# A ConvNeXt V2 block on one core: zero rows appended to the expansion matmul, and rstd transposed on VectorE instead of TensorE

## The chip, the core and the metric

The kernel runs on one core of a Trainium2 chip. The metric is device time in microseconds (us), lower is better. Engines are named as in the profile: PE is TensorE's matrix multiplication, PEld its weight loads, DVE is VectorE, ACT is ScalarE, POOL is GpSimd, SP is SyncE, and SPq is SP's sequencer, which issues most of the DMAs here. PEclk, or "the granted clock", is the share of full speed that TensorE's clock was granted: 0.5 is called cold here, 1.0 warm.

## The reference

One image of 512 x 512 pixels and 96 channels goes through a depthwise 3x3 convolution, a LayerNorm over channels, an expansion to 384, a GELU, a global response normalization (GRN) and a projection back.

```python
# x (1,512,512,96), dw (3,3,96), w1 (96,384), w2 (384,96), all bf16
out = depthwise_conv3x3(x, dw)                      # padding 1
h = _layernorm(out, axis=-1)                        # over the 96 channels
h = gelu(h @ w1)                                    # tanh form
gx = sqrt((h * h).sum(axis=(1, 2), keepdims=True) + 1e-6)
nx = gx / (gx.mean(axis=-1, keepdims=True) + 1e-6)
h = grn_gamma * (h * nx) + grn_beta + h
return x + h @ w2
```

GRN needs sums over the whole image, so the kernel has two phases: the first computes everything up to the GELU and its sums, the second projects. The change is in the first phase.

## The kernel before

The first phase works in slots, one block of four image rows per slot and 128 in all. These are the parts that matter (cuts are marked `# ...`).

Convolution, eviction and squares of block b. ACT evicts the nine-tap result and POOL squares it:

```python
nc.tensor.matmul(Y[32*j:32*j+32, i, ...], lhsT=Wd[32*i:32*i+32, t, :], rhs=xT[32*i:32*i+32, ...], ...)
# ...
nc.scalar.activation(out=y[:], in_=Y[:], func=ACTF.Identity)                # y_bf
nc.gpsimd.tensor_tensor(out=q[:], in0=y[:], in1=y[:], op=ALU.mult)          # ysq
```

LayerNorm statistics. Two slots later PE sums y (12 matmuls) and then the squares (12 matmuls) into one PSUM tile S per batch of eight blocks. After the eighth block DVE turns S into rstd by a chain of some 15 small operations, PE transposes rstd, DVE copies it out, and SP writes it to DRAM and reads it back broadcast over partitions (rbc):

```python
for src, h in ((ybf[b], 0), (ysq.pop(b), 1)):
    # ...
    nc.tensor.matmul(S[:, h, ...], lhsT=src[:, i, g*128:(g+1)*128], rhs=rowsel[:], ...)
# ... stage_chain(k): mean, nmsq, var, ri, three Newton steps (t_, rn) on DVE, then
nc.tensor.matmul(S[:N, 2, :], lhsT=rn[:, :N], rhs=ident_bf[:], start=True, stop=True)
nc.vector.tensor_copy(out=rt[:N, :], in_=S[:N, 2, :])
nc.sync.dma_start(out=r_dram[...], in_=rt[:N, :])
# ... stage_bcast(k), one slot later: 4 DMAs  rbc <- r_dram
```

Normalization and expansion. POOL multiplies by rstd, SP writes the result to DRAM and reads it transposed (ynT), PE expands it, ACT applies the GELU, and DVE collects the sums for GRN:

```python
nc.gpsimd.tensor_tensor(out=yn[:], in0=ybf.pop(b)[:], in1=rbcs[k][...].to_broadcast(...), op=ALU.mult)
nc.sync.dma_start(out=yn_dram[b], in_=yn[:]...)
# ...
for i in range(2):
    nc.tensor.matmul(U[:, i, :], lhsT=w1p[:, j*128:(j+1)*128], rhs=ynts[b][:, i0+i, :], start=True, stop=True)
nc.scalar.activation(out=perm_view(gt[:, :], i0, 2), in_=perm_src(U[:]), func=ACTF.Gelu_apprx_tanh)
# ... nc.vector.bn_stats(...) on gt
```

The schedule puts the statistics LAG_ST = 2 slots after the convolution, the norms LAG_NORM = 4 slots after a batch's last statistics, and the expansion LAG_MLP = 3 slots after the norm. Every sixteenth slot has a burst of filler matmuls, meant to warm the clock (`fill_tiles(7)`). A compile-time scheduler orders each engine's instructions within the limits of their dependencies, so the order on POOL and SP is not always that of the text.

Of the kernel before, what the change touches and what calls it, by code (L numbers as in the profile page):

```python
# [19 lines left out]
LAG_MLP = 3  # L20
FILL_FIRST = 16
FILL_EARLY = 6
REWARM = 16


def batches_of(nblk):
# [13 lines left out]
def kernel(  # L40
# [46 lines left out]
    def yn_src(q):  # L87

        return yn_dram[q].rearrange("(r c) (i w) -> c i r w", r=GR, i=NI).rearrange("c i r w -> (c i) r w")
# [41 lines left out]
    nc.vector.memset(ones_f[:], 1.0)  # L131
    eps_t = consts.tile([128, 1], f32, name="eps_t")
    nc.vector.memset(eps_t[:], GRN_EPS)
    w1p = consts.tile([C, E], bf16, name="w1p")
    with tc.tile_pool(name="w1ps", bufs=1, space=bass.MemoryType.PSUM) as w1ps, \
            tc.tile_pool(name="w1tmp", bufs=1) as w1tmp:
        cen = w1tmp.tile([C, C], bf16, name="cen")
        nc.vector.memset(cen[:], 1.0)
        w1m = w1ps.tile([C, E], f32, name="w1m")
        nc.tensor.matmul(w1m[:], lhsT=cen[:], rhs=w1_raw[:], start=True, stop=True)  # L140
        nc.vector.scalar_tensor_tensor(out=w1p[:], in0=w1m[:], scalar=-1.0 / C, in1=w1_raw[:],
                                       op0=ALU.mult, op1=ALU.add)

    NACC = (NBLK + 7) // 8
# [24 lines left out]
    def recompute_units(q, pspool, uname):  # L169
        if not is_recomp(q) or q in done_recomp:  # L170
            return []
        gts, ynt = grp[q]["gts"], grp[q]["ynt"]
        units = []
        for i0 in range(0, GR, 2):
            for j in range(NCH):
                def unit(i0=i0, j=j):
                    U = pspool.tile([128, 2, W], f32, name=uname)
                    for i in range(2):
                        nc.tensor.matmul(U[:, i, :], lhsT=w1p[:, j * 128:(j + 1) * 128],  # L179
                                         rhs=ynt[:, i0 + i, :], start=True, stop=True)  # L180
                    nc.scalar.activation(out=perm_view(gts[j][:, :], i0, 2), in_=perm_src(U[:]),  # L181
                                         func=ACTF.Gelu_apprx_tanh)
                units.append(unit)
        return units
# [4 lines left out]
    with ExitStack() as p1:  # L189
# [4 lines left out]
        rtpool = p1.enter_context(tc.tile_pool(name="rt", bufs=2))  # L194
        rbcpool = p1.enter_context(tc.tile_pool(name="rbc", bufs=3))
        ynpool = p1.enter_context(tc.tile_pool(name="yn", bufs=3))
        yntpool = p1.enter_context(tc.tile_pool(name="ynt", bufs=4))
        gpool = p1.enter_context(tc.tile_pool(name="g", bufs=7))
        bstpool = p1.enter_context(tc.tile_pool(name="bst", bufs=2))
        psY = p1.enter_context(tc.tile_pool(name="psY", bufs=1, space=bass.MemoryType.PSUM))  # L200
# [61 lines left out]
        def stage_stats(b):  # L262
            k = batch_of[b]
            b0, n = BATCHES[k]
            if b == b0:
                Ss[k] = psS.tile([128, 3, 128], f32, name="S")
            S = Ss[k]
            for src, h in ((ybf[b], 0), (ysq.pop(b), 1)):
                for g in range(NG):
                    c0 = (b - b0) * GR * NG + g  # L270
                    for i in range(NI):
                        nc.tensor.matmul(S[:, h, c0:c0 + (GR - 1) * NG + 1:NG],  # L272
                                         lhsT=src[:, i, g * 128:(g + 1) * 128], rhs=rowsel[:],
                                         start=(i == 0), stop=(i == NI - 1))

        def stage_chain(k):
            b0, n = BATCHES[k]
            N = n * GR * NG
            S = Ss[k]
            mean = small.tile([128, 128], f32, name="mean")  # L280
            nc.vector.tensor_scalar(out=mean[:, :N], in0=S[:, 0, :N], scalar1=1.0 / C, scalar2=None, op0=ALU.mult)
            nmsq = small.tile([128, 128], f32, name="nmsq")
            nc.vector.scalar_tensor_tensor(out=nmsq[:, :N], in0=mean[:, :N], scalar=-1.0, in1=mean[:, :N],  # L283
                                           op0=ALU.mult, op1=ALU.mult)
            var = small.tile([128, 128], f32, name="var")
            nc.vector.scalar_tensor_tensor(out=var[:, :N], in0=S[:, 1, :N], scalar=1.0 / C, in1=nmsq[:, :N],
                                           op0=ALU.mult, op1=ALU.add)
            nc.vector.tensor_scalar(out=var[:, :N], in0=var[:, :N], scalar1=0.0, scalar2=LN_EPS,
                                    op0=ALU.max, op1=ALU.add)
            ri = small.tile([128, 128], i32, name="ri")  # L290
            nc.vector.tensor_scalar(out=ri[:, :N], in0=var[:, :N].bitcast(i32), scalar1=1, scalar2=None,  # L291
                                    op0=ALU.arith_shift_right)
            nc.vector.tensor_scalar(out=ri[:, :N], in0=ri[:, :N], scalar1=-1, scalar2=0x5F3759DF,
                                    op0=ALU.mult, op1=ALU.add)
            rcur = ri[:, :N].bitcast(f32)
            rn = None
            for it in range(NEWTON_ITERS):
                t_ = small.tile([128, 128], f32, name="nt")
                nc.vector.scalar_tensor_tensor(out=t_[:, :N], in0=rcur, scalar=-0.5, in1=rcur,  # L299
                                               op0=ALU.mult, op1=ALU.mult)  # L300
                nc.vector.tensor_tensor(out=t_[:, :N], in0=t_[:, :N], in1=var[:, :N], op=ALU.mult)  # L301
                rn = small.tile([128, 128], bf16 if it == NEWTON_ITERS - 1 else f32,
                                name="rstd" if it == NEWTON_ITERS - 1 else "rn")
                nc.vector.scalar_tensor_tensor(out=rn[:, :N], in0=t_[:, :N], scalar=1.5, in1=rcur,  # L304
                                               op0=ALU.add, op1=ALU.mult)
                rcur = rn[:, :N]

            nc.tensor.matmul(S[:N, 2, :], lhsT=rn[:, :N], rhs=ident_bf[:], start=True, stop=True)  # L308
            rt = rtpool.tile([128, 128], bf16, name="rt")
            nc.vector.tensor_copy(out=rt[:N, :], in_=S[:N, 2, :])  # L310
            nc.sync.dma_start(out=r_dram[b0:b0 + n].rearrange("b r (g m) -> (b r g) m", g=NG), in_=rt[:N, :])
            Ss.pop(k)

        def stage_bcast(k):
            b0, n = BATCHES[k]
# [12 lines left out]
            nc.sync.dma_start(out=yn_dram[b], in_=yn[:].rearrange("p i w -> p (i w)"))  # L328

        def stage_read(b):  # L330
            t = yntpool.tile([C, GR, W], bf16, name="ynT")
            nc.sync.dma_start(out=t[:], in_=yn_src(b))
            ynts[b] = t

        bsts = {}
# [43 lines left out]
            for m in range(n):  # L379
                nc.tensor.matmul(U[:, m % 2, :], lhsT=zero[:, :128], rhs=zero[:], start=True, stop=True)  # L380

        def fill_tiles(n):
            U = psU.tile([128, 2, W], f32, name="U")
            for m in range(n):
                for i in range(2):
                    for j in range(4):
                        nc.tensor.matmul(U[32 * j:32 * j + 32, i, :], lhsT=zero[32 * i:32 * i + 32, :32],  # L387
                                         rhs=zero[32 * i:32 * i + 32, :], start=True, stop=True)


        at = {}

# [5 lines left out]
        for k, (b0, n) in enumerate(BATCHES):  # L398
            for b in range(b0, b0 + n):
                s = b + LAG_ST  # L400
                if b == b0:
                    s = max(s, last_stat_slot + 2)
                put(max(s, b + LAG_ST), ("stats", b))
                last_s = max(s, b + LAG_ST)
            last_stat_slot = last_s
            put(last_s, ("chain", k))
            put(last_s + 1, ("bcast", k))
            for b in range(b0, b0 + n):
                s = max(last_norm + 1, last_s + LAG_NORM)
                last_norm = s  # L410
                put(s, ("norm", b))
                put(s + 2, ("read", b))
                put(s + LAG_MLP, ("mlp", b))
                last_slot = s + LAG_MLP
                if b % 8 == 7 or b == NBLK - 1:
                    put(s + LAG_MLP, ("combine", b // 8))
# [4 lines left out]
        for s in range(last_slot + 1):  # L421
# [7 lines left out]
                stage_bcast(k)  # L429
            for b in get("norm"):  # L430
                stage_norm(b)
            units = []
            for b in get("mlp"):
                units += mlp_units(b)
# [7 lines left out]
            if not u:  # L442
                order += t
                if t:
                    order.append(lambda: fill(FILL_EARLY))
                order += stats
            elif s % REWARM == REWARM - 1 and t:
                order += u[:2] + t + [lambda: fill_tiles(7)] + u[2:4] + stats + u[4:]
            else:
                k = 0  # L450
                while u or t:
                    if u:
                        order.append(u.pop(0))
                    n = 2 - k % 2
                    order += t[:n]
                    t = t[n:]
                    if k == 1:
                        order += stats
                    k += 1
# [126 lines left out]
```

## Time and profile before

| | before |
|---|---|
| time, median of 2 runs | 2130.15 us (2129.92 to 2130.39) |
| profiled span, mean granted clock | 2121.6 us, 0.660 |
| first phase ends (start of the GRN sums) | 1536.7 us |
| second phase | 584.9 us (2121.6 less 1536.7) |
| mean expansion matmul | 610 ns |

These lines of the profile page are the span and three rows of the slices. The span is cut into 40 equal slices, and each digit is the busy share of a slice in tenths, or for PEclk the granted clock in tenths.

```profile
span 2121.6 us, 59634 instructions
...
PE   7888999999999999999999989998579999999998
...
DVE  4465767867776786777678677779968888888887
...
PEclk8576555555555555555555575555589999999999
```

For three quarters of the time PE is about 90% busy at half clock, while DVE has room. One line of the windows view, for the stretch from 200 to 1150 us of the first phase, gives it in numbers. Its columns are the stretch, its length, busy time of PE, PEld, DVE, ACT and POOL (with instructions), the granted clock, the DMA share and GB/s.

```profile
200.00:1150.00 950.00, 907.86 (x12058) 245.70 (x12058) 698.07 (x1228) 594.70 (x571) 473.93 (x164) 0.50 0.66 178
```

PE is busy 908 of 950 us at exactly half clock. These are three groups of instructions from the page: line, engine, operation, output and inputs, shapes and count, then busy time and the mean ns of one, then the engine's idle time before them and what ended it.

```profile
L355 DVE BATCH_NORM_STATS2 bst<-gt 128x6 f32<-128x512 bf16 x1536 | 944.8, 679 | 364.2 <-ACT gt L352 364.2
...
L347 PE MATMUL U<-ynT,w1p 96*128 96x512 bf16 x1536 | 755.7, 610 | 19.4 <-ACT gt L352 18.2
...
L257 POOL TENSOR_TENSOR ysq<-y_bf 128x1536 bf16<-128x1536 bf16 x128 | 351.9, 2751 | 584.4 <-ACT y_bf L254 584.4
```

The expansion uses 96 of the array's 128 rows ("96*128"). A square takes POOL 2.75 us, and a norm takes it 3.09 us.

The only long waits of PE in the first phase are for rstd, once per batch: the waits view has 17 of them, 81.6 us in total, the longest 9.2. The PE timeline shows one of them (start, duration, instruction, and in brackets the idle time before it and its cause):

```profile
1237.43 0.60 PE L347 MATMUL U<-ynT,w1p 96*128 96x512 bf16 x2
1247.21 0.29 PE L308 MATMUL S<-ident_bf,rstd 128*128 128x128 bf16 x1 [9.18 <-DVE rstd L304]
```

PE started no other matmul in between, so everything behind the transpose stood for 9.18 us.

### The profile page before, as it was taken

Reading aid. Unit: us, or ns where it says so; the run is one execution under the profiler, and the core shown is the slowest. Engines: PE = TensorE matmul, PEld = TensorE weight load, DVE = VectorE, ACT = ScalarE, POOL = GpSimd, SP = SyncE. Lnnn points to the kernel's source line nnn. Section 1 sums busy time; section 2 is a strip of 40 time slices with the busy share of each in tenths; the row PEclk is TensorE's granted clock in tenths of the full one; section 3 lists DMA queues with packets and bytes.
Section 4 is the critical chain, followed back from the end, with each engine's and each line's share of the span. In section 5 each row is a group of like instructions: output and inputs, shape, how many; then the busy total and the mean of one; then the engine's idle time right before and its main releaser. Section 6 shows DMA issues by size and latency. Waiting matters only on the chain.

```text
span 2121.6 us, 59634 instructions
## 1 busy us (share of the span) xinstructions
PE 1925.0 (91%) x26046; PEld 776.0 (37%) x26046; DVE 1588.6 (75%) x2645; ACT 1395.9 (66%) x1381; POOL 850.1 (40%) x463
## 2 busy tenths in 40 slices
PE   7888999999999999999999989998579999999998
PEld 3433222232222223222222322232156666666665
DVE  4465767867776786777678677779968888888887
ACT  1464666665666666566666666678568787878787
POOL 4537445373644537364453745624021111111110
PEclk8576555555555555555555575555589999999999
DMA  8668666674866667476665868436199999999996
GB/s 159 184 144 219 166 180 163 173 204 127 222 163 189 158 175 209 122 225 157 194 159 170 209 161 220 145 123 218 69 350 364 371 367 371 365 375 366 374 363 232
DMA packets 459861, 472.21 MB, mean 223 GB/s; under 512 B 285424, under 2 KB 381776, under 8 KB 459600
## 3 DMA queue, kind: packets, MB, share of 16 engines
q1 hardware_dynamic: 406992, 348.85, 56.7%
q0 software_dynamic: 20608, 88.09, 11.2%
q10 hardware_dynamic: 32000, 31.46, 4.8%
q8 instruction: 203, 3.33, 0.7%
q14 instruction: 58, 0.48, 0.1%
HBM read 224.55 MB, written 176.69 MB: 189 GB/s over the span
## 4 chain that ended last, share of the span: by engine, by line
PE 62%; DVE 17%; ACT 14%; DMA 3%; POOL 2%; issue 1%; SPq 0%; ACTq 0%; DVEq 0%; POOLq 0%
PE U L347 25%; PE Y L244 21%; ACT gl L181 12%; DVE bst L355 10%; PE O L535 8%; PE S L272 3%; DMA out_dram<-o_sb 2%; DVE rstd L304 2%; ACT gt L352 1%; POOL yn L326 1%; DVE nmsq L283 1%; PE U L387 1%; DVE nt L301 1%; DVE nt L299 1%; DVE ri L291 1%
## 5 line engine op out<-in xcount | busy, mean ns | idle before, releaser
L355 DVE BATCH_NORM_STATS2 bst<-gt 128x6 f32<-128x512 bf16 x1536 | 944.8, 679 | 364.2 <-ACT gt L352 364.2
L352 ACT ACTIVATE gt<-U 128x1024 bf16<-128x1024 f32 x768 | 770.3, 1027 | 478.1 <-PE U L347 346.5
L347 PE MATMUL U<-ynT,w1p 96*128 96x512 bf16 x1536 | 755.7, 610 | 19.4 <-ACT gt L352 18.2
L244 PE MATMUL Y<-xT,Wd 32*32 32x512 bf16 x13806 | 587.2, 587 | 3.3 <-DMA xT<-in_x_dram 2.8
L257 POOL TENSOR_TENSOR ysq<-y_bf 128x1536 bf16<-128x1536 bf16 x128 | 351.9, 2751 | 584.4 <-ACT y_bf L254 584.4
L326 POOL TENSOR_TENSOR yn<-y_bf,rbc 128x1536 bf16<-128x1536 bf16 x128 | 392.3, 3089 | 130.3 <-DMA yn_dram<-yn 75.4
L535 PE MATMUL O<-W2s,gl 128*128 128x96 bf16 x6096 | 350.4, 206 | 19.7 <-ACT gl L181 5.1
L535 PEld LDWEIGHTS <-gl 128*128 128x128 bf16 x6096 | 304.2, 97 | 140.3 <-ACT gl L181 54.0
L537 DVE TENSOR_TENSOR o_sb<-O,xb 128x384 bf16<-128x384 f32 x512 | 257.3, 552 | 100.1 <-PE O L535 98.2
L244 PEld LDWEIGHTS <-Wd 32*32 32x32 bf16 x13806 | 156.0, 101 | 434.6 <-issue 411.8
L347 PEld LDWEIGHTS <-w1p 96*128 96x128 bf16 x1536 | 130.0, 117 | 477.8 <-issue 471.2
L165 POOL DMA_DIRECT2D xr<-in_x_dram x127 | 68.6, 541 | 496.8 <-DVE xb L526 373.2
L254 ACT ACTIVATE y_bf<-Y 128x1536 bf16<-128x1536 f32 x128 | 185.0, 1445 | 99.8 <-PE Y L244 99.8
L526 DVE TENSOR_TENSOR xb<-xr,B2bc_f 128x1536 f32<-128x1536 bf16 x127 | 222.9, 1755 | 10.6 <-DMA xr<-in_x_dram 7.9
L179 PEld LDWEIGHTS <-w1p 96*128 96x128 bf16 x960 | 76.7, 98 | 88.6 <-issue 72.9
L272 PEld LDWEIGHTS <-y_bf 128*128 128x128 bf16 x1536 | 66.3, 108 | 60.0 <-issue 58.6
L308 PE MATMUL S<-ident_bf,rstd 128*128 128x128 bf16 (+2 forms) x18 | 5.2, 290 | 81.6 <-DVE rstd L304 81.6
L272 PE MATMUL S<-rowsel,ysq 128*128 128x4 bf16 x1536 | 59.7, 168 | 8.1 <-POOL ysq L257 7.6
L272 PE MATMUL S<-rowsel,y_bf 128*128 128x4 bf16 x1536 | 63.5, 170 | 1.1 <-issue 1.1
L272 PEld LDWEIGHTS <-ysq 128*128 128x128 bf16 x1536 | 51.0, 103 | 10.1 <-POOL ysq L257 7.9
L159 POOL DMA_DIRECT2D gl<-g_dram x71 | 37.6, 533 | 6.4 <-DVE W2s L500 3.6
L308 PEld LDWEIGHTS <-rstd 128*128 128x128 bf16 (+2 forms) x18 | 1.9, 108 | 95.1 <-DVE rstd L304 94.8
(1123 smaller groups left out, 1079.0 us busy)
## 6 DMA issues: line engine op xcount, KB each, us to landing
g_dram<-gt SPq DMA_DIRECT2D x144, 512.0 KB, 3.8
yn_dram<-yn SPq DMA_DIRECT2D x128, 384.0 KB, 4.0
ynT<-yn_dram SPq DMA_DIRECT2D x128, 384.0 KB, 4.2
out_dram<-o_sb SPq DMA_DIRECT2D x128, 384.0 KB, 6.7
xr<-in_x_dram POOLq DMA_DIRECT2D x127, 384.0 KB, 7.0
gl<-g_dram POOLq DMA_DIRECT2D x71, 512.0 KB, 8.9
gl<-g_dram SPq DMA_DIRECT2D x70, 512.0 KB, 8.7
ynl<-yn_dram ACTq DMA_DIRECT2D x80, 384.0 KB, 9.9
```

What stands on the lines that cost most here:

```text
L181: nc.scalar.activation(out=perm_view(gts[j][:, :], i0, 2), in_=perm_src(U[:]), func=ACTF.Gelu_apprx_tanh)
L244: nc.tensor.matmul(Y[32 * j:32 * j + 32, i, oc0:oc1], lhsT=Wd[32 * i:32 * i + 32, t, :], rhs=xT[32 * i:32 * i + 32, r % XR, oc0 + dx:oc1 + ...
L254: nc.scalar.activation(out=y[:], in_=Y[:], func=ACTF.Identity)
L257: nc.gpsimd.tensor_tensor(out=q[:], in0=y[:], in1=y[:], op=ALU.mult)
L272: nc.tensor.matmul(S[:, h, c0:c0 + (GR - 1) * NG + 1:NG], lhsT=src[:, i, g * 128:(g + 1) * 128], rhs=rowsel[:], start=(i == 0), stop=(i == ...
L326: nc.gpsimd.tensor_tensor(out=yn[:], in0=ybf.pop(b)[:], in1=rbcs[k][:, b - b0:b - b0 + 1, :].to_broadcast([128, NI, W]), op=ALU.mult)
L347: nc.tensor.matmul(U[:, i, :], lhsT=w1p[:, j * 128:(j + 1) * 128], rhs=ynts[b][:, i0 + i, :], start=True, stop=True)
L352: nc.scalar.activation(out=perm_view(gt[:, :], i0, 2), in_=perm_src(U[:]), func=ACTF.Gelu_apprx_tanh)
L355: nc.vector.bn_stats(out=bst[:, j, (b % 8) * GR + m, :], in_=gt[:, m * W:(m + 1) * W])
L526: nc.vector.tensor_tensor(out=xb[:], in0=xr[:], in1=B2bc_f[:, None, :].to_broadcast([128, PXP, C]), op=ALU.add)
L535: nc.tensor.matmul(O[:, gl_, :], lhsT=gts[j][:, gg * 128:(gg + 1) * 128], rhs=W2s[:, j, :], start=(j == 0), stop=(j == NCH - 1))
L537: nc.vector.tensor_tensor(out=o_sb[:, sub * GPS:(sub + 1) * GPS, :], in0=O[:], in1=xb[:, sub * GPS:(sub + 1) * GPS, :], op=ALU.add)
```

## The change

The intent: keep the clock warm by using all 128 rows of the array in the expansion (32 rows of zeros on both operands, so the result stays the same), take the transpose and its wait away from PE, and drop the bursts, which a warm clock would not need.

```diff
-REWARM = 16
-    w1p = consts.tile([C, E], bf16, name="w1p")
+    w1p = consts.tile([128, E], bf16, name="w1p")
+    nc.vector.memset(w1p[C:128, :], 0.0)
 ...
+        for i in range(NYT):                       # NYT = 4, a ring in place of a pool
+            t = yntpool.tile([128, GR, W], bf16, name=f"ynT{i}")
+            nc.gpsimd.memset(t[C:128, :, :], 0.0)
+            yn_ring.append(t)
 ...
-            nc.tensor.matmul(S[:N, 2, :], lhsT=rn[:, :N], rhs=ident_bf[:], start=True, stop=True)
-            nc.vector.tensor_copy(out=rt[:N, :], in_=S[:N, 2, :])
-            nc.sync.dma_start(out=r_dram[b0:b0 + n]..., in_=rt[:N, :])
+            nc.vector.transpose(out=rt[:, :NT], in_=rn[:, :NT])     # within 32x32 squares
+        def stage_rows(k):
+                for a in range(4):
+                    nc.sync.dma_start(out=dst[:, 32 * a:32 * a + 32].rearrange("(t q) p -> q t p", q=32),
+                                      in_=rt[32 * a:32 * a + 32, ...].rearrange("q (t p) -> q t p", p=32))
 ...
-            put(last_s + 1, ("bcast", k))
+            put(last_s + 1, ("rows", k))
+            put(last_s + 2, ("bcast", k))
 ...
-            elif s % REWARM == REWARM - 1 and t:
-                order += u[:2] + t + [lambda: fill_tiles(7)] + u[2:4] + stats + u[4:]
```

The second phase still passes 96 rows (`w1p[:C, ...]`).

## The prediction

> **What bounds the kernel now.** The page's slices show two phases: up to 1535 us the granted TensorE clock is mostly 0.5 with PE 90% busy; then (587 us, untouched) 0.9-1.0 with DMA 0.98. From 200 to 1400 us PE limits: in the PE timeline a slot (one 4-row block) repeats every 10.84 us without a gap: 12 expansion matmuls and nine convolution taps at about 0.43 us each, 0.86 us of statistics and switching. In the same slots ACT needs about 7.6 us (six 1.02 us GELUs, one 1.44 us eviction), DVE about 8.5 us (592 us busy from 400 to 1200 us, about 69.5 slots).
>
> **Why it is cold.** [...] the eight rises of the clock fall on a 3.413 us grid. And PE was gap-free for most of 201-1219 us at 96 rows and never warmed, so occupancy is not what counts. By my estimate (columns streamed times share of the array used) clean windows of the steady mix reach about 67%; windows that warmed are pure convolution[...] or contain 128-row fillers (77-85%). Of seven periodic bursts one (1215 us) warmed. That warmth died at 1242 us, when PE stood 9.2 us waiting for the rstd transpose behind the DVE chain. Such waits (waits view) total 81.6 us in 17 places.
>
> **What the change does.**
> - 128 rows: same matmul duration, but the mix's estimated activity outside statistics rises from 67% to 79%, above what warmed. The clock should rise, and again after each loss.
> - No TensorE transpose: 81.6 us of PE waits go[...]. The DVE transpose replaces a 0.27 us copy.
> - No bursts: 21.6 us of fillers go.
> - Costs: rstd rows go in 64 B pieces and the broadcast one slot later. The next batch's statistics still wait until DVE has read the single S buffer; with DVE behind, PE may stall there, and SP on the rstd rows.
>
> **Sum.** Warm PE needs (estimate) 5.5 us per slot, so DVE becomes the limit: 8.5 us instead of 11.5 (10.84 plus waits and bursts, averaged over 400-1200). About 113 slots from 200 us on save up to 3 us each, 340 us; the last 12 (1405-1517) are already DVE-bound, leaving about 300. I subtract 35 for DVE starvation, cold windows, S stalls, and DMA share rising from 0.66 to 0.8. Phase 1 ends near 1270 instead of 1535; total about **1865 us**, range 1790 to 1985. If the clock stays at 0.5, only waits and bursts go: about 2030. Chances: faster 0.95, same 0.04, slower 0.01.
>
> **Right or wrong in the profile.** Right: clock 0.9-1.0 in nearly all of phase 1; no PE wait on rstd; DVE near 95% busy from 200 us on; the expansion matmul's mean falls from 610 to near 400 ns; second phase unchanged. Wrong: clock 0.5 with PE gap-free (rows do not weigh, or zeros do not count); clock oscillating, with PE waits[...] at a batch's first statistics matmul (on DVE's var), or on ynT or rbc.
>
> **What would make it wrong.** Padding not counting; warmth lost each batch through DVE lag; SP's queue blocked by the rstd rows, delaying xT, yn and g; DMA contention; POOL (5.8 us per slot) slowed by, or slowing, a busier DVE.

The sum: 340 less the last slots is about 300, less 35 is 265, and 2130 less 265 is 1865. Its 5.5 us per warm slot is an estimate, about half of the 10.84 us measured at clock 0.50. The eight rises are in the windows view of the kernel before, at 17.1, 41.0, 61.5, 126.3, 177.5, 198.0, 1218.6 and 1553.1 us; a grid of 3.413 us fits them within 0.12 us, and its steps are the "windows" of the text. The estimate of 67% and 79% follows from its timeline: twelve expansion matmuls on 96 of 128 rows and nine taps (each twelve 32*32 matmuls, 75% of 128*128), about 0.42 us each, in the 9.98 us of a slot outside statistics and switching: 21 x 0.42 x 0.75 / 9.98 = 66%, and 79% with 128 rows in the expansion. Pure convolution comes to 75% in the same way. That the clock follows such a share was assumed; the runs below test only the rows.

## More of the kernel before

Next, three lines of the waits view: who waited for whom, total us, number of waits, longest.

```profile
PE S L308 <- DVE rstd L304: 81.6, 17, 9.2
...
POOL yn L326 <- DMA rbc<-r_dram: 54.6, 3, 41.2
...
PE S L272 <- POOL ysq L257: 7.6, 4, 2.8
```

## The result, and the profile after

| | before | after |
|---|---|---|
| time, median of 2 runs | 2130.15 us | 2010.43 us (2009.78 to 2011.09) |
| profiled span, mean granted clock | 2121.6 us, 0.660 | 2008.0 us, 0.865 |
| first phase ends | 1536.7 us | 1424.4 us |
| second phase | 584.9 us | 583.6 us |

The ratio is 0.9438, 95% interval 0.9397 to 0.9479. All ratios are the mean time of a kernel's fast runs over the mean of the fast runs of the kernel before from the same rounds, so they are not quite the ratios of the medians quoted.

The change saved 5.6%, all of it in the first phase, but about 145 us less than predicted. The same lines of the page after:

```profile
span 2008.0 us, 58620 instructions
...
PE   7675766757667586675766757566399999999998
...
DVE  3454779889798897988979889799788888888887
...
PEclk9787878879788797887978879787699999999999
```

```profile
200.00:1150.00 950.00, 642.02 (x12896) 242.56 (x13078) 816.23 (x1356) 643.31 (x634) 528.45 (x183) 0.82 0.72 196
```

The clock did warm, to a mean of 0.82 in the stretch, but it swings: the digits go up and down through the whole first phase. PE is busy only 642 of 950 us, and no engine took its place as the limit (DVE has 86%). Something makes all of them wait. The groups and waits say what:

```profile
L372 DVE BATCH_NORM_STATS2 bst<-gt 128x6 f32<-128x512 bf16 x1536 | 929.5, 676 | 228.6 <-ACT gt L369 228.3
...
L279 PE MATMUL S<-rowsel,ysq 128*128 128x4 bf16 x1536 | 58.9, 167 | 337.0 <-POOL ysq L264 335.1
...
L364 PE MATMUL U<-ynT_160,w1p 128*128 128x512 bf16 x327 | 118.4, 435 | 16.0 <-ACT gt L369 15.0
```

```profile
PE S L279 <- POOL ysq L264: 335.1, 46, 14.6
...
POOL yn L343 <- DMA rbc<-r_dram: 285.6, 18, 32.8
```

The wait for rstd is gone from PE (81.6 us before). In its place PE waits 335 us for the squares (7.6 before), and POOL waits 286 us for the broadcast rstd (54.6 before). The timelines of one batch show how these two belong together. First PE and POOL:

```profile
830.63 0.44 PE L279 MATMUL S<-rowsel,y_bf 128*128 128x4 bf16 x12
843.52 0.48 PE L279 MATMUL S<-rowsel,ysq 128*128 128x4 bf16 x12 [12.45 <-POOL ysq L264]
```

```profile
837.67 3.08 POOL L343 TENSOR_TENSOR yn<-y_bf,rbc 128x1536 bf16<-128x1536 bf16 x1 [17.40 <-DMA rbc<-r_dram]
840.72 2.75 POOL L264 TENSOR_TENSOR ysq<-y_bf 128x1536 bf16<-128x1536 bf16 x1
843.42 9.20 POOL L343 TENSOR_TENSOR yn<-y_bf,rbc 128x1536 bf16<-128x1536 bf16 x3
```

PE did the sums of y at 830.63 and needed the square of the same block. The compile-time order had put a norm ahead of that square, and in this trace POOL ran them in that order: the norm stood 17.40 us for rbc, so the square ran only behind it, at 840.72, and PE stood 12.45 us.

Why was rbc so late? DVE in the same batch, with one of POOL's squares set between (it comes from POOL's timeline) and the BATCH_NORM_STATS2 and most of the small operations left out, and then SP:

```profile
806.43 0.27 DVE L289 TENSOR_SCALAR mean<-S 128x128 f32<-128x128 f32 x1
...
810.42 0.29 DVE L307 SCALAR_TENSOR_TENSOR nt<-ri 128x128 f32<-128x128 f32 x1
810.44 2.88 POOL L264 TENSOR_TENSOR ysq<-y_bf 128x1536 bf16<-128x1536 bf16 x1 [4.38 <-ACT y_bf L261]
810.75 2.72 DVE L309 TENSOR_TENSOR nt<-nt,var 128x128 f32<-128x128 f32 x1
...
822.73 0.29 DVE L317 STREAM_TRANSPOSE rt<-rstd 128x128 bf16<-128x128 bf16 x1
```

```profile
823.05 2.28 SPq L327 DMA_DIRECT2D r_dram<-rt  x4
825.42 4.28 SPq L223 DMA_TRANSPOSE xT<-in_x_dram  x1
829.89 1.91 SPq L335 DMA_DIRECT2D rbc<-r_dram  x4
```

From the start of the chain to the norm is 31.2 us (806.43 to 837.67). The chain takes 16.6 us of it. The operations themselves are 0.2 to 0.3 us each, but three groups of GRN's statistics (about 2.46 us each) are queued between them, and two of the operations took 2.72 us. Each of those began beside a square on POOL (810.44 to 813.32 for the one shown) and ended just after it. So it is 2.72 us beside the square, where the same operation of the next Newton step took 0.29 us (814.15), with no POOL instruction running. The statistics were not slowed in this way: five that ran from 803.47 on, beside the square of 803.31 to 806.06, took 3.05 us together, 0.61 each (their mean over the run is 676 ns). Why the one kind is slowed and the other is not was not shown. Then 2.28 us go to issuing the rows, 4.28 us to an image load (over the run 3.73 to 7.94 us, median 4.98) that stands between them and the broadcast on SP's queue, and the rest to issue and landing.

In the warm part of this batch PE repeats a slot every 7.06 us (801.95, 809.01, 816.07, 823.13 and 830.20 start the same matmul of consecutive slots). LAG_NORM leaves four slots: 4 x 10.84 = 43 us cold, but 28 us warm. The latency of 31 us fits into the first and not into the second.

The compile-time order left less than that. The norm reached the head of POOL's queue at 820.27 (837.67 less the wait of 17.40), only 13.8 us after the chain began. The program puts the batch's first norm behind the squares of the blocks that ACT evicted at 822.98 and 830.04; the compiled order put it ahead of both. By estimate, in the program's place it could have started at 834.2 at the earliest (830.04, plus 1.45 for the eviction and 2.75 for the square), and would have waited about 3 us for rbc instead of 17. Two windows show what the wait does to the clock:

```profile
791.00:832.00 41.00, 35.99 (x791) 14.79 (x790) 38.59 (x70) 40.14 (x41) 11.14 (x4) 1.00 0.68 167
832.00:849.00 17.00, 5.12 (x88) 1.56 (x90) 14.73 (x25) 2.96 (x4) 11.32 (x4) 0.51 1.00 273
```

While warm the kernel is paced by ACT (40.14 of 41 us). Then PE stalls for 12.45 us and the clock falls to half (1.00 in the first window, 0.51 in the second). A batch takes 83.7 us (half of the 167.36 us between the rstd rows issued at 739.71 and at 907.07) where eight warm slots would take 56.5 (8 x 7.06).

So there were two theories to test. A: the rows warm the clock, and the fixed latency of rstd plus POOL's order take much of it back. The rival: the rows matter little, and what was gained came from PE no longer waiting for rstd.

### The profile page after: what moved, and what is told of

Its sections match the earlier page's. It is cut to its first block, busy times and chain, and to the rows that moved or that the text cites. A ratio compares the mean times of both kernels' runs of the same rounds, so it can differ in the third digit from the quotient of the medians.

```text
span 2008.0 us, 58620 instructions
## 1 busy us (share of the span) xinstructions
PE 1461.1 (73%) x25394; PEld 730.8 (36%) x25636; DVE 1626.7 (81%) x2646; ACT 1374.0 (68%) x1381; POOL 856.8 (43%) x467
## 4 chain that ended last, share of the span: by engine, by line
PE 29%; POOL 18%; ACT 18%; DVE 12%; issue 10%; DMA 8%; another core or an unknown queue 2%; SPq 2%; ACTq 0%; POOLq 0%; DVEq 0%
POOL yn L343 14%; ACT gl L182 14%; DVE bst L372 9%; PE O L545 9%; PE Y L251 8%; PE U L364 7%; DMA rbc<-r_dram 5%; POOL ysq L264 5%; ACT y_bf L261 3%; ACT gt L369 1%; SPq L335 1%; PE U L397 1%; DVE sq L388 1%; DMA out_dram<-o_sb 1%
## 5 line engine op out<-in xcount | busy, mean ns | idle before, releaser
L372 DVE BATCH_NORM_STATS2 bst<-gt 128x6 f32<-128x512 bf16 x1536 | 929.5, 676 | 228.6 <-ACT gt L369 228.3
L369 ACT ACTIVATE gt<-U 128x1024 bf16<-128x1024 f32 x768 | 750.1, 1032 | 418.8 <-remote 217.0
L343 POOL TENSOR_TENSOR yn<-y_bf,rbc 128x1536 bf16<-128x1536 bf16 x128 | 392.0, 3089 | 285.6 <-DMA rbc<-r_dram 285.6
L251 PE MATMUL Y<-xT,Wd 32*32 32x512 bf16 x13806 | 419.4, 430 | 54.3 <-issue 15.5
L364 PEld LDWEIGHTS <-w1p 128*128 128x128 bf16 x1536 | 113.8, 100 | 366.8 <-issue 336.9
L251 PEld LDWEIGHTS <-Wd 32*32 32x32 bf16 x13806 | 144.8, 91 | 277.1 <-issue 256.7
L364 PE MATMUL U<-ynT_160,w1p 128*128 128x512 bf16 x327 | 118.4, 435 | 16.0 <-ACT gt L369 15.0
L364 PE MATMUL U<-ynT_158,w1p 128*128 128x512 bf16 x327 | 115.9, 425 | 17.7 <-ACT gt L369 16.5
L364 PE MATMUL U<-ynT_162,w1p 128*128 128x512 bf16 x325 | 115.8, 428 | 16.4 <-ACT gt L369 15.4
L364 PE MATMUL U<-ynT_156,w1p 128*128 128x512 bf16 x325 | 109.1, 407 | 19.3 <-ACT gt L369 12.0
L180 PEld LDWEIGHTS <-w1p 96*128 96x128 bf16 x960 | 76.7, 98 | 88.3 <-issue 72.5
L279 PEld LDWEIGHTS <-y_bf 128*128 128x128 bf16 x1536 | 56.2, 96 | 35.8 <-issue 7.1
L388 DVE SCALAR_TENSOR_TENSOR sq<-bst 128x64 f32<-128x64 f32 x48 | 59.0, 1231 | 1.4
```

The lines of the kernel that those rows point to most:

```text
L251: nc.tensor.matmul(Y[32 * j:32 * j + 32, i, oc0:oc1], lhsT=Wd[32 * i:32 * i + 32, t, :], rhs=xT[32 * i:32 * i + 32, r % XR, oc0 + dx:oc1 + ...
L279: nc.tensor.matmul(S[:, h, c0:c0 + (GR - 1) * NG + 1:NG], lhsT=src[:, i, g * 128:(g + 1) * 128], rhs=rowsel[:], start=(i == 0), stop=(i == ...
L364: nc.tensor.matmul(U[:, i, :], lhsT=w1p[:, j * 128:(j + 1) * 128], rhs=ynts[b][:, i0 + i, :], start=True, stop=True)
L372: nc.vector.bn_stats(out=bst[:, j, (b % 8) * GR + m, :], in_=gt[:, m * W:(m + 1) * W])
```

## The experiments

Unless noted, edits are to the kernel after. "First phase" is its end in the profiled run. The kernel before had medians of 2125 to 2130 us beside them, and all kernels gave correct results.

| run | median us | ratio (95% interval) | mean clock | first phase |
|---|---|---|---|---|
| after | 2010.43 | 0.9438 (0.9397 to 0.9479) | 0.865 | 1424.4 |
| e1_lag6 | 1975.9 | 0.9309 (0.9250 to 0.9368) | 0.876 | 1403.1 |
| e2_rows96 | 2054.98 | 0.9677 (0.9616 to 0.9738) | 0.661 | 1469.8 |
| e3_before_rows128 | 1976.71 | 0.9307 (0.9236 to 0.9377) | 0.872 | 1390.7 |
| e4_lag6_rows96 | 2033.48 | 0.9581 (0.9518 to 0.9643) | 0.674 | 1463.1 |
| e5_order | 1916.87 | 0.9033 (0.8981 to 0.9086) | 0.885 | 1331.4 |
| e6_order_lag6 | 1923.25 | 0.9054 (0.8997 to 0.9112) | 0.874 | 1346.1 |
| e7_squares_on_act | 1794.45 | 0.8451 (0.8404 to 0.8499) | 0.946 | 1204.4 |
| e8_before_rows_order_lag6 | 1851.1 | 0.8714 (0.8653 to 0.8774) | 0.909 | 1273.1 |
| e9_rows_late | 1850.6 | 0.8728 (0.8661 to 0.8795) | 0.879 | 1277.6 |
| e10_squares_act_rows_pool | 1819.65 | 0.8588 (0.8528 to 0.8648) | 0.933 | 1235.6 |
| e11_squares_act_rows96 | 2019.09 | 0.9526 (0.9465 to 0.9588) | 0.667 | 1432.6 |
| e12_before_rows_squares_act | 1833.7 | 0.8656 (0.8594 to 0.8718) | 0.931 | 1248.7 |
| e13_rows128_no_bursts | 1967.47 | 0.9288 (0.9217 to 0.9360) | 0.871 | 1378.9 |
| e14_bcast_with_rows | 2009.21 | 0.9476 (0.9415 to 0.9538) | 0.864 | 1419.6 |
| e15_rows97 | 2054.45 | 0.9692 (0.9630 to 0.9754) | 0.664 | 1468.5 |
| e16_bcast_adjacent | 1981.76 | 0.9316 (0.9295 to 0.9336) | 0.869 | 1396.4 |
| e17_squares_act_bcast_adjacent | 1826.81 | 0.8582 (0.8558 to 0.8606) | 0.936 | 1243.1 |

### Do the rows warm the clock?

**e2_rows96** keeps everything of the change but the rows:

```diff
-    nc.tensor.matmul(U[:, i, :], lhsT=w1p[:, j * 128:(j + 1) * 128], rhs=ynts[b][:, i0 + i, :], ...)
+    nc.tensor.matmul(U[:, i, :], lhsT=w1p[:C, j * 128:(j + 1) * 128], rhs=ynts[b][:C, i0 + i, :], ...)
```

> The changed kernel with the expansion back on 96 rows (the zero rows stay in memory but are not streamed). If the rows used are what warms the clock: clock 0.5 for nearly all of 200 to 1400 us and about 2030 us (2010 to 2060), the gain of removed waits and bursts alone. If removing the PE waits on the transpose was what kept the clock warm and the rows do not matter: 2010 us as with the whole change, clock above 0.8.

The window of the stretch is this, and the next one is that of **e15_rows97**, which uses `[:C + 1]` in the same two places, that is, 97 rows, one of them zeros:

```profile
200.00:1150.00 950.00, 938.45 (x12532) 252.08 (x12520) 745.07 (x1298) 627.52 (x605) 515.44 (x179) 0.50 0.68 189
```

> The whole change with 97 rows in the expansion, one more than the 96 of the run that stayed cold. If single rows are counted: cold, clock near 0.5, about 2055 us as with 96. If a group of 32 rows counts whole once one of its rows is used: warm as with 128, clock above 0.8 in the first phase, about 2010.

```profile
200.00:1150.00 950.00, 937.61 (x12473) 251.98 (x12474) 745.53 (x1299) 628.47 (x605) 515.26 (x179) 0.50 0.68 189
```

Both are cold. PE was busy 99% of the stretch (in e2 it had two waits of over 3 us in it, both before 217 us), and still got half clock; with 128 rows and 68% busy it got 0.82. So the rows do warm the clock, occupancy alone does not, and the rival is wrong about the clock. One row more than 96 is not enough (0.50 with 97): that a group of 32 rows counts whole, the second guess of the expectation, was not borne out. Where between 97 and 128 the border lies was not tried. How the saving of the whole change divides depends on what is taken away first: without PE's wait for rstd and without bursts, but on 96 rows, the time falls from 2130 to 2055, and the rows add only 45 us to that (2055 to 2010); added alone to the kernel before, they save some 150 (e3, next). Why only 45 in the whole change is the question for the rest.

**e3_before_rows128** is the kernel before with the rows alone (the w1p and ynT parts of the diff; TensorE transpose and bursts stay), and **e13_rows128_no_bursts** is e3 without the bursts:

> The kernel before with only the 128-row expansion added (TensorE transpose, bursts and broadcast slot as before). If the rows alone bring the gain: 2010 us within 20. If the transposes on TensorE cost the warmth at every batch (a wait of about 9 us each): clock oscillating, and 2030 to 2080 us.

> The kernel before with 128 rows and without the periodic bursts (TensorE transpose kept). If the missing bursts are what makes the whole change slower than the rows alone: 2000 to 2020 us. If the bursts are idle weight once the rows warm the clock (21 us of PE work, PE not the limit when warm): 1955 to 1985.

The rows alone reach 1977 us, and 1967 without bursts. That is better than the whole change. The bursts bring nothing (without them it is 9 us faster, but the two intervals overlap); the other half of the change, the moved transpose, costs some 33 to 43 us (2010 less 1977 or 1967, in rounds of different calls). None of the theories had said so. The waits view of e3:

```profile
PE S L279 <- POOL ysq L264: 148.0, 36, 12.4
PE S L315 <- DVE rstd L311: 145.2, 18, 10.7
...
POOL yn L333 <- DMA rbc<-r_dram: 48.0, 5, 34.8
```

Between e3 and the whole change, PE trades 145 us of waiting for rstd against 187 us more of waiting for squares (335 less 148). My reading is that PE's wait on rstd acts as a brake, which holds the slots back until rstd is there; without it PE runs ahead, and the wait returns one step later, where POOL's order makes it longer. The transpose is not all that differs between the two, though: in the traces of e3 and of the kernel before, POOL runs the eight norms of a batch in runs of 3, 1 and 4 between squares; the compile of the whole change put them in runs of 1, 3 and 4, with the first norm alone, ahead of a square.

### More time for rstd, or another order on POOL?

**e1_lag6** and **e4_lag6_rows96** give the norms six slots instead of four, with 128 and with 96 rows:

```diff
-LAG_NORM = 4
+LAG_NORM = 6
```

> The changed kernel with the norm stage six slots after the statistics instead of four (LAG_NORM 4 to 6; nothing else). Theory A (latency): warm slots last 7.1 us, so four slots are 28 us, but the rstd takes 35 us from the first DVE operation of its chain to the landed broadcast; GpSimd stalls on it and holds ysq, PE and the clock. Six slots (42 us or more) cover it: about 1850 us (1820 to 1890), GpSimd's waits on rbc fall from 286 us to under 60, clock above 0.95 from 200 us to the end of the first phase. Theory B (VectorE is already the limit at 85-89% busy[...]): no more than 1.5% gained, 1980 to 2010 us.

> Both: 96 rows and a lag of six. Theory A: with cold slots of 10.8 us four slots (43 us) already cover the 35 us, so the lag is worth nothing here: within 10 us of the 96-row run. If the lag helps for another reason than slots having become short, it gains here too, 50 us or more.

With 128 rows this gained 35 us, far less than theory A wanted, and PE still waited 260.6 us for squares; the compile had also given POOL another order, norms in runs of 3 and 5. With 96 rows it gained 21 us, between the two expectations (within 10, or 50 and more). So latency is a part, not the whole.

**e5_order** and **e6_order_lag6** pin POOL's program order, one norm and one square per slot, with lag 4 and 6:

```diff
-    nc.gpsimd.tensor_tensor(out=q[:], in0=y[:], in1=y[:], op=ALU.mult)
+    tc.keep_in_program_order(nc.gpsimd.tensor_tensor(out=q[:], in0=y[:], in1=y[:], op=ALU.mult))
-    nc.gpsimd.tensor_tensor(out=yn[:], ...)
+    tc.keep_in_program_order(nc.gpsimd.tensor_tensor(out=yn[:], ...))
```

> The changed kernel with GpSimd's instructions held in the order in which the kernel's source emits them, so one norm (yn) and one square (ysq) per slot instead of runs of three to five norms ahead of the next square; lag still four. Theory A (only the latency of rstd to broadcast): the 17 us wait on rbc per batch stays and so does the time, 1990 to 2020 us. Theory C (the runs of norms in front of the squares, which PE's statistics wait for, cost the rest): PE's waits on ysq fall from 335 us to under 200 us and the time to 1930 to 1975.

> The same fixed order and a lag of six. Theories A and C together: GpSimd's waits on rbc under 60 us, PE's on ysq under 40 us, clock above 0.95 from 200 us to the end of the convolution, VectorE near 95% busy, 1850 us (1820 to 1890). If VectorE or the DMA was the limit behind them: above 1920 with the clock high. If latency is not what is left: the clock still oscillates, 1950 or more.

The order alone gained 94 us (2010 to 1917), more than expected; the waits for squares left the top of the list. POOL's wait for rbc nearly went too, with the lag still four (285.6 us in the changed kernel, and here):

```profile
POOL yn L343 <- DMA rbc<-r_dram: 29.4, 5, 19.5
```

So the long wait came mostly from the place that the compiled order gave the norms, and not from a lag of four slots as such. One reservation: PE's new waits, which come next, also give rstd more time. The lag on top of it gained nothing (1923), against the expectation. New waits had come up. In e5 PE waits 92.0 us in 12 for DVE's var, that is, for S to come free (the prediction had named this one), and 155 us for ynT. In e6 PE's largest wait is the one for ynT:

```profile
PE U L364 <- DMA ynT<-yn_dram: 165.2, 22, 15.8
```

ynT is read over SP's queue. In SP's own waits of e6 the write of the rstd rows stands 186.9 us in 16, the longest 15.7 us, for DVE's transpose; everything behind it on that queue (yn, ynT, image loads) stands as well: in one batch SP issued nothing between 828.59 and 842.65.

**e9_rows_late** is e6 with the rows issued at `last_s + 3` and the broadcast at `last_s + 4`, and with the row DMAs pinned there (the norms come at `last_s + 6`):

> The fixed-order, lag-six version with the four small writes of rstd issued two slots later (slot 3 instead of 1 after the statistics; broadcast in 4 instead of 2), so that SP meets them when VectorE has finished. Theory D (in the 1923 us run SP stands 187 us at these writes, up to 15.7 us, and the writes and reads of yn behind them come late, so PE waits 165 us for ynT and loses the clock): SP's wait on rt under 60 us, PE's waits on ynT under 60 us, 1840 to 1890 us. If SP's standing is not what delays ynT: within 15 us of 1923.

It hit: 1851 us, 73 us less than e6. SP's wait for the transpose left the top of its list, and the ynT line became:

```profile
PE U L364 <- DMA ynT<-yn_dram: 65.6, 16, 9.7
```

**e8_before_rows_order_lag6** is the kernel before with the rows, the pinned POOL order and lag 6, that is, e6 with the TensorE transpose and the bursts:

> The kernel before (TensorE transpose, bursts) with 128 rows, the fixed GpSimd order and a lag of six. It differs from the fixed-order, lag-six version of the changed kernel in the transpose, the bursts and the broadcast slot. If the TensorE transpose costs PE about 9 us and the warmth in each of some 15 batches: 50 to 100 us slower than that version. If VectorE is the limit anyway: within 20 us of it.

It was expected to be slower than e6 and was 72 us faster (1851 against 1923), though PE waited 178.7 us for rstd in it. SP stood only 55.7 us for rt there (186.9 in e6), which fits the brake. Issued late, the DVE transpose is as good (e9, 1851); issued as in the change, it is worse.

### Which part of the way of rstd costs?

**e14_bcast_with_rows** issues the broadcast in the same slot as the rows, `last_s + 1`, as before the change:

> The whole change with the broadcast issued right behind the rstd writes in the same slot, ahead of the next load of x (which took SP 4.3 us between the two). If the late broadcast makes GpSimd wait: its wait on rbc falls from 286 us by 60 to 100, and the time to 1970 to 2000. If only the chain on VectorE and the runs of norms matter: within 10 us of 2010.

Nothing changed (2009). But its trace shows that it had not done what it was meant to do. The compile-time order again put the image load between the rows and the broadcast:

```profile
816.54 2.02 SPq L327 DMA_DIRECT2D r_dram<-rt  x4
818.99 4.05 SPq L223 DMA_TRANSPOSE xT<-in_x_dram  x1
823.22 1.92 SPq L335 DMA_DIRECT2D rbc<-r_dram  x4
```

**e16_bcast_adjacent** therefore pins image loads, rows and broadcasts in program order as well:

```diff
-    nc.sync.dma_start_transpose(dst[:, 0:npix_t], src)
+    tc.keep_in_program_order(nc.sync.dma_start_transpose(dst[:, 0:npix_t], src))
# the same around the four row DMAs and the four broadcasts
```

> As the broadcast-slot run, but the image loads, the rows of rstd and the broadcasts keep program order on SP's queue, so the broadcast is issued right after the rows. In both earlier kernels with the DVE transpose the image load (4.1 to 4.3 us to issue) stood between the two, so the broadcast-slot run did not take it away. The PE and DVE orders are those of the changed kernel; GpSimd's norms come as runs of 3, 1 and 4 instead of 1, 3 and 4. A: the part of the 33 to 43 us that the moved transpose costs comes from the longer way of rstd through SP's queue: the norms start about 5 us sooner in each of the 17 batches, GpSimd's wait on rbc falls from 286 by 60 to 90 us, and the time falls to 1950 to 1985. B: the broadcast is not what the statistics wait for (the order of norms and squares on GpSimd is): the wait on rbc falls, PE's wait on the squares stays above 300 us, and the time stays within 1990 to 2020.

```profile
804.56 1.74 SPq L327 DMA_DIRECT2D r_dram<-rt  x4
809.42 1.78 SPq L335 DMA_DIRECT2D rbc<-r_dram  x4
```

The time hit A's range: 1982 us, 29 us less than after. But it does not show that the way through SP's queue was the cause. The way became only a little shorter: from the start of DVE's chain to the issue of the broadcast it is 21.2 us here (median of the batches from 400 to 1150 us), 23.1 in the changed kernel and 15.6 in e3, because SP now stands for the rows to land before it issues the broadcast (35.4 us in 23 waits, 5.8 in the changed kernel). POOL's wait for rbc did not fall as far as its own line says either:

```profile
POOL yn L343 <- DMA rbc<-r_dram: 133.8, 10, 32.8
...
POOL yn L343 <- DMA g_dram<-gt: 99.3, 7, 16.1
```

A norm does not read g_dram. These seven waits stand before the first norm of a batch, where the one for rbc belongs; the profile put them down to another DMA. Together they are 233 us, 52 less than 285.6 and not the 60 to 90 that A wanted. And the pins also changed POOL's order back to that of e3 (norms in runs of 3, 1 and 4 instead of 1, 3 and 4 between squares), while PE's wait on squares stayed at 321.4 us, in 34 waits instead of 46, as B had said of it. The run does not separate the two.

### Taking the squares off POOL

**e7_squares_on_act** lets ACT square, right after its eviction:

```diff
-    nc.gpsimd.tensor_tensor(out=q[:], in0=y[:], in1=y[:], op=ALU.mult)
+    nc.scalar.activation(out=q[:], in_=y[:], func=ACTF.Square)
```

> The changed kernel with the squares for the statistics on ScalarE (activation Square of y_bf) instead of GpSimd, nothing else. PE then waits for no GpSimd instruction before its statistics. If GpSimd's queue is what stalls PE (A and C): PE's wait on ysq below 30 us and at least 60 us gained, 1870 to 1950, although ScalarE takes 1.45 us more per slot (8.5 us, about what VectorE needs). If the stalls come from elsewhere: 2000 or more, since ScalarE has more to do.

This was better than its expected range: 1794 us, 15.5% less than before, and it beats both kernels. The page and the window:

```profile
PEclk9799989999999899899898999868999999999999
...
L279 PE MATMUL S<-rowsel,ysq 128*128 128x4 bf16 x1536 | 57.5, 166 | 5.1 <-issue 4.1
```

```profile
200.00:1150.00 950.00, 713.64 (x14438) 292.93 (x14629) 866.73 (x1653) 897.57 (x872) 343.48 (x113) 0.95 0.89 233
```

The wait for the squares fell from 337 to 5.1 us of idle time, although ACT got 1.49 us more work per slot. The clock is 0.95, with PE 75% busy. POOL's norms now wait longer than before (711 us; 270.6 of them put down to rbc, most of the others to g_dram or gt, which a norm does not read), but no square stands behind them. ACT is 94% and DVE 91% busy: these are now the limit, with a slot every 8.7 us (872 instructions of ACT in 950 us, eight to a slot). Over the whole run DVE is busy 1503 us instead of 1627 with the same work, which fits fewer of its operations meeting a POOL instruction: one of GRN's small operations (`sq<-bst`) took 1231 ns on average after the change and 339 here. How the 216 us (2010 to 1794) divide between the freed queue and the faster DVE was not tested; e5, which left the squares on POOL, gained 94 by the order alone.

**e11_squares_act_rows96** is e7 with 96 rows, and **e12_before_rows_squares_act** is the kernel before with the rows and with squares on ACT:

> Squares on ScalarE with the expansion on 96 rows. With the stalls gone, this measures the clock alone: if 96 rows leave it at 0.5, slots of 10.8 us and about 2030 us (2000 to 2060), so the rows are worth some 240 us here against 45 us in the changed kernel. If the clock warms without the rows, under 1900.

> The kernel before (TensorE transpose, bursts) with 128 rows and squares on ScalarE. It differs from the 1794 us run in the transpose, the bursts and the broadcast slot. If the TensorE transpose stops PE some 10 us in every batch and costs the clock: 1840 to 1900, so the change's other half is worth 50 to 100 us once GpSimd is out of the way. If VectorE is the limit either way: within 20 us of 1794.

With 96 rows it is cold again (0.50 in the stretch, with PE busy all of its 950 us) and takes 2019 us. So with the stalls away the rows are worth 225 us (2019 less 1794), while in the whole change they were worth 45. With the TensorE transpose and the bursts it takes 1834 us: here the rest of the change gains 39 us, where it lost 33 to 43 before. The sign of the moved transpose depends on whether the statistics queue behind the norms on POOL.

**e10_squares_act_rows_pool** moves the row and broadcast DMAs of e7 to POOL's queue, and **e17_squares_act_bcast_adjacent** adds the pins of e16 to e7:

> Squares on ScalarE, and the writes of rstd and its broadcast issued from GpSimd's queue, where only the norms that need them come after. With theory D: SP's 63 us on rt go and the clock stays above 0.95; VectorE and ScalarE then limit, so only 10 to 40 us below the 1794 us run: 1755 to 1785. If GpSimd's issue of the transfers costs more than SP's wait did: 1800 or more.

> The same pins on the version with the squares on ScalarE, where nothing on GpSimd holds the statistics up. Both theories: within 1 per cent of 1794 (1775 to 1810), since the norms have slack there (GpSimd under 40 per cent busy in the first phase); if it falls below 1775, the way of rstd was still limiting.

Both missed and were slower, 1820 and 1827. In e10 POOL waits 443 us for DVE's transpose at the head of its queue, with the norms behind it, so the blocking was moved, not removed. In e17 the norms' wait is no shorter (752 us instead of 711, whatever it is put down to), and SP's image loads now wait 341 us in all (298 in e7), mostly for PE, with the rest of the queue behind them. That these waits make the 32 us was not shown.

## Why the prediction was right or wrong

- **"The clock should rise, and again after each loss"**: right. e2 and e15 show that it is the rows that do it, as the prediction argued from the 96-row stretches.
- **"No TensorE transpose: 81.6 us of PE waits go"**: these waits went, but longer ones came: in place of 81.6 us for rstd PE stood 335 us for the squares, which it met next.
- **"DVE becomes the limit: 8.5 us"** per slot: the rate was within reach, and e7 averages 8.7 us. The change itself averaged 10.5 us (83.7 us per batch of eight), 7.06 us while warm (there ACT set the pace, busy 40.14 of 41 us) and much longer in the stalls. DVE was 86% busy in the stretch, not the predicted 95%.
- **"I subtract 35 for DVE starvation, cold windows, S stalls, and DMA share"**: this is the step that failed. The gross saving was put at 300 us and the first phase shrank by 112.3 (1536.7 less 1424.4), so the term came out at 188 us, not 35. (The gross figure was within reach: in e7, without the stalls, the first phase shrank by 332 us.) Its mechanism was listed ("clock oscillating") but given little weight, and the wait was put at var, ynT or rbc. rbc was right for POOL; PE's own wait was for the squares behind it. The prediction counted POOL's 5.8 us per slot as load, but did not look at the order of POOL's instructions, in which squares stood behind norms, nor at the four slots of LAG_NORM, which shrink from 43 to 28 us when the clock warms and of which the compiled order left 14.
- **"Clock 0.9-1.0 in nearly all of phase 1"**: wrong, 0.82 in the stretch.
- **"The expansion matmul's mean falls from 610 to near 400 ns"**: 407 to 435 ns for the four buffers. Right.
- **Second phase unchanged**: 584.9 and 583.6 us. Right.
- **"SP's queue blocked by the rstd rows"** was named as a risk and was real: e6 against e9 shows 73 us of it.

The predicted 1865 us was close to what the change can give without the stalls; with the squares on ACT it gives 1794.

What stays open: how the 33 to 43 us of the moved transpose divide between the way of rstd and the norms' order on POOL (e16 changed both), where between 97 and 128 rows the clock warms, and why the pins make e17 slower.

## What to carry to other kernels

When a change speeds up the engine that sets the pace, list the waits that are fixed in microseconds (here rstd's 31 us) and compare them with the slack, which is given in slots and shrinks with them; read the slack from the compiled order, not from the program (here 14 us were left of 28); then look at what stands behind those waits on the same engine or DMA queue (here squares behind norms on POOL, 335 us of PE's waits). Work that the fast engine needs soon should not share a queue with work that waits for a long latency: moving 1.5 us of squares to an already busier engine gained 216 us here (2010 to 1794). A wait that looks like waste can be a brake that keeps a longer one away, so test the parts of a change one by one.
